# Linear attention followed by an ELU feed-forward layer: batch 0 laid out in slots of two heads by nine tokens, its small matmuls on the array's diagonal quarters, and new orders of work for every batch

## The chip, the cores and the metric

The kernel runs on one core of a Trainium2 chip. The metric is the device time of one launch in microseconds (us). A core has a matrix engine (PE, with its weight loads shown apart as PEld), three engines for elementwise work (DVE, ACT, POOL), a queue engine that issues transfers (SP; ACT and POOL issue some too), and 16 DMA engines that all queues share. Each engine works through its own instructions in program order and waits at a semaphore where an operand is not ready.

## What is computed

The inputs are `q`, `k`, `v` of shape (8 batches, 8 heads, 576 tokens, 64) and two weight matrices of 512x2048 and 2048x512, all float32.

```python
q_s = softmax(q, over the 64 features of a token)
k_s = softmax(k, over the 576 tokens of a head)
kv  = einsum('bhsd,bhse->bhde', k_s, v)          # 64x64 per head
x   = einsum('bhsd,bhde->bhse', q_s, kv)         # put back to (8*576, 512)
h   = x @ w_in
out = where(h > 0, h, exp(min(h, 0)) - 1) @ w_out
```

## The kernel before

**The feed-forward layer** runs in nine rounds of 16 steps. Rounds 0 to 7 take 512 tokens of one batch each; round 8 takes the 64 tokens that each batch has over. A step `(j, s)` issues `hidden` (four matmuls of 128x512 into a bank, L778; exp on ACT, L766; minus one on POOL, L767), `project` of the step three before it (four matmuls, L799) and `elu` (max and min on DVE, L789), in that order. A step with nothing else in it takes 8 matmuls.

**The attention** of batch j+1 is cut into words, and the tables `FIRST` (round 0), `SECOND` (round 1), `LATER` and `CHANGED` put words between the steps: `mid` words behind `hidden`, `end` words behind `project`, `after` words behind `elu`. For q: `qmax` and `qsum` (DVE reductions, L586 and L604, with a reciprocal, L606), `qsub` (subtract, L594), `qexp` (ACT, L600), `qmul` (L618), a transpose (`pturn` on PE, L652, or `turn` by DMA, L634) and `pwide`/`wide` (copy to `QT`, L670, L733). For k: a maximum over tokens, `ksub` (L414, L425), `kexp` (L452). `vconv` casts v (L515). `kv` multiplies (L535, L539), `kfac` divides into `MB` (L552, L566), `att` or `flat` multiplies `MB` with `QT` (L687, L709) and `xc` or `xflat` copies the result to `XT`, which `hidden` of the next round reads. `hold` lets SP wait for the last `hidden` matmul.

**Maxima of k.** From batch 2 on `peak2` (DVE, L367, L374) and `join2` reduce them, and `kout2`/`kin` send them through a scratch tensor in DRAM to all partitions (`NB`). Batch 1 is done otherwise: `kmax2` at the end of `START` (DVE, L299 to L312), then `kturn` (PE, L328), `kacross`, `diag`, `kspread` (PE, L431) and `copy` in round 0. Batch 0, before any feed-forward work can start, goes by the word list `START`: `kraw` copies k into banks by matmuls with the identity (L462, L471), `kmin` adds the negative maxima (L479, L488), `kexp` reads the banks (L502). `warm` issues four matmuls whose result is not used (L924). At its end `h:2:4` and `h:0:2` issue the first two matmuls of the first four steps.

**Layout.** A partition holds four neighbouring tokens of every head, 512 tokens in all (parts A and B, four heads each); the other 64 tokens (part R) lie apart, and are loaded by descriptors of 256 bytes, reduced, transposed and multiplied by words of their own (`qmulr`, `turn:R`, `wide:R`, `rest0`, `rcopy0`). Each `store` of a round sends four tiles of 128 rows; `store_rest` sends round 8.

**Queues.** SP issues the loads in the order of the words; POOL issues `w1` and `w2`, the weight loads. Only `hold` and `await` (L962) keep SP back, else it runs ahead and the transfers queue up.

Of the kernel before, what the change touches and what calls it, by code (L numbers as in the profile page):

```python
# [4 lines left out]
ALU = mybir.AluOpType  # L5
# [12 lines left out]
SR = S - SM  # L18
CUTS = (0, 320, 832, 1344, 1856, 2304)
# [6 lines left out]
EARLY = 4  # L26
OB = (3, 4, 5, 6)
# [19 lines left out]
FIRST = {  # L47
    0: ("", "", ""),
    1: ("", "", ""),
    2: ("qmax:A", "w2:6:8", ""),  # L50
    3: ("qsub:0 w1:12:14", "qsub:1:dve", ""),
    4: ("", "qmax0:R qexp:A w2:8:12", "qsum:A load:Q:1:B qsub0:R"),
    5: ("", "kturn kacross", "qexp0:R qmul:A qsum0:R"),
    6: ("diag", "qmax:C", ""),
    7: ("qsub:D:dve", "kspread qsub:2 w1:14:16", "hold copy load:V:1:RAB"),
    8: ("qexp:C", "qmulr0:gp ksub:1:dve", "ksub:0:dve load:K:2:MR"),
    9: ("pturn:A", "ksub:3 ksub:R", "qsum:C pwide:A:act"),
    10: ("qmul:B:dve pturn0:R kexp:A", "pwide0:R:act", ""),
    11: ("vconv:A:dve", "rest0 w2:12:13 vconv:R", "ksub:2:dve rcopy0:act"),
    12: ("load:Q:2:ABR pturn:B kexp:R vconv:B:gp", "", "load:V:2:MR pwide:B:act"),  # L60
    13: ("kv:A", "kexp:B kfac:A:dve att:0", "xc:0 w2:13:15 w2:15:16 peak2:A"),
    14: ("kv:B kfac:B:dve", "att:1 qmulr:dve peak2:B", "xc:1"),
    15: ("peak2:R join2 att:3 xc:3", "", "turn:R att:2 xc:2 kout2"),
}
SECOND = {
    0: ("qmax:A", "qsub:0:dve qmax:C", "load:Q:2:MR qsub:1"),
    1: ("qexp:A", "qsub:D", ""),
    2: ("qsub:2", "", ""),
    3: ("kin qsum:A", "qmul:0", "qexp:C wide0:R:act"),
    4: ("", "qsum:C", "qmul:1:dve ksub:2:dve"),  # L70
    5: ("", "load:K:2:MR", ""),
    6: ("qmulr:dve ksub:R:dve", "kexp:R qmul:B:dve", "ksub:3:dve"),
    7: ("rest0 turn:A", "rcopy0:dve", "vconv:B"),
    8: ("", "vconv:R ksub:A", "kexp:B peak2:B"),
    9: ("peak2:R kexp:A", "vconv:A:dve", "turn:R peak2:A"),
    10: ("", "", "turn:B join2"),
    11: ("", "kv:AB", "wide:A:gp"),
    12: ("kfac:AB:dve", "wide:R:act", ""),
    13: ("wide:B:gp", "flat:0", "xflat:0:act"),
    14: ("flat:1", "load:V:2:MR xflat:1:dve flat:2", "xflat:2:act"),  # L80
# [36 lines left out]
class Gen:  # L117
# [173 lines left out]
    def kmax(self, b, part, en="dve"):  # L291
# [743 lines left out]
```

## Time and profile before

| what | us |
|---|---|
| median of 3 runs (310.12 to 311.53) | 311.34 |
| the profiled execution | 311.08 |
| its span, first to last instruction | 309.3 |
| first feed-forward matmul (`h:2:4`) | 20.74 |
| first `project` matmul | 26.17 |
| round 0's step 4 begins | 27.20 |
| rounds 1, 2, 3, 4, 5 begin | 55.66, 88.22, 119.95, 151.25, 182.54 |
| last `project` matmul ends | 306.06 |

The profiled execution is 1.8 us longer than its span: what lies around the first and last instruction. A round's beginning is the start of its first L778 matmul on the timeline of PE. In rows of the profile a group has its line, engine, operation, tiles, shapes, count, then busy time and the mean of one, then the idle time of its engine before it and who ended it.

### The profile page before, as it was taken

How to read it: one execution, taken by the hardware profiler on the slowest of the kernel's cores; microseconds unless marked ns; L12 is line 12 of the kernel's file. 1: busy time of each engine (PE TensorE's matmuls, PEld its weight loads, DVE VectorE, ACT ScalarE, POOL GpSimd, SP SyncE). 2: the span in 40 equal slices, each digit the busy share in tenths (PEclk: the TensorE clock that was granted, in tenths of full speed). 3: DMA queues.
4: the chain of work that ended last, by engine and by line, in shares of the span. 5: the costliest groups of instructions: out<-in, count | busy, mean ns of one | idle time of the engine just before them, and what ended most of it. 6: DMA issues, size and time to landing. Idle time of an engine off the chain costs nothing.

```text
span 309.3 us, 4546 instructions
## 1 busy us (share of the span) xinstructions
PE 296.4 (96%) x1601; PEld 237.0 (77%) x1601; DVE 241.8 (78%) x420; ACT 177.3 (57%) x295; POOL 173.6 (56%) x229
## 2 busy tenths in 40 slices
PE   4888998999999999999999999999999999999995
PEld 1456875788878888888888888788888888888884
DVE  6999998999969998999799979997995354335441
ACT  1475785567456755694569547855695543334432
POOL 2988985575546754675467546763676333333440
PEclk9999999999999999999999999999999999999999
DMA  7999999999407986756565666561512030003003
GB/s 238 317 352 328 372 335 306 255 290 236 153 12 228 264 199 159 217 142 179 170 215 145 173 177 200 156 156 44 170 36 42 2 136 0 0 2 137 0 1 136
DMA packets 65607, 51.63 MB, mean 167 GB/s; under 512 B 29360, under 2 KB 58288, under 8 KB 65584
## 3 DMA queue, kind: packets, MB, share of 16 engines
q1 hardware_dynamic: 57984, 41.23, 48.9%
q0 software_dynamic: 6400, 8.39, 10.3%
q10 hardware_dynamic: 1200, 1.72, 1.8%
q8 instruction: 12, 0.20, 0.3%
q14 instruction: 11, 0.09, 0.1%
HBM read 38.27 MB, written 9.45 MB: 154 GB/s over the span
## 4 chain that ended last, share of the span: by engine, by line
PE 86%; DMA 6%; DVE 4%; SPq 1%; ACT 1%; issue 0%; POOL 0%; DVEq 0%
PE bank L778 41%; PE bank L799 40%; DMA KR<-in_k_dram 6%; PE bank L709 2%; PE bank L535 1%; PE bank L687 1%; DVE QZ L604 1%; SPq L276 1%; SPq L284 1%; DVE KA L299 1%; DVE QM L586 0%; DVE KM L367 0%; DVE QS L618 0%; DVE DG L355 0%; DVE MB L566 0%
## 5 line engine op out<-in xcount | busy, mean ns | idle before, releaser
L767 POOL TENSOR_SCALAR ES<-ES 128x512 f32<-128x512 f32 x144 | 95.8, 666 | 118.1 <-ACT ES L766 118.1
L799 PE MATMUL bank<-W2S,GT 128*128 128x512 f32 x576 | 154.7, 392 | 0.9 <-DVE GT L789 0.9
L778 PE MATMUL bank<-XT,W1S 128*128 128x512 f32 x512 | 139.2, 394 | 0.2 <-ACT XT L696 0.2
L789 DVE SCALAR_TENSOR_TENSOR GT<-bank,ES 128x512 fp32r<-128x512 f32 x144 | 96.5, 678 | 50.2 <-PE bank L778 41.5
L766 ACT ACTIVATE ES<-bank 128x512 f32<-128x512 f32 x144 | 85.4, 597 | 86.5 <-PE bank L778 85.8
L799 PEld LDWEIGHTS bank<-W2S,GT 128*128 128x128 f32 x576 | 107.2, 188 | 23.7 <-DVE GT L789 1.4
L778 PEld LDWEIGHTS bank<-XT,W1S 128*128 128x128 f32 x512 | 94.2, 188 | 19.6 <-ACT XT L696 0.9
L594 POOL TENSOR_TENSOR QR<-QR,QM 128x512 f32<-128x512 f32 (+3 forms) x24 | 28.7, 1197 | 5.4 <-DVE QM L586 5.2
L600 ACT ACTIVATE QR<-QR 128x1024 f32<-128x1024 f32 (+3 forms) x18 | 19.0, 1061 | 12.6 <-POOL QR L594 11.3
L586 DVE TENSOR_REDUCE QM<-QR 128x16 f32<-128x1024 f32 (+3 forms) x18 | 21.7, 1207 | 0.6 <-DMA QR<-in_q_dram 0.5
L604 DVE TENSOR_REDUCE QZ<-QR 128x16 f32<-128x1024 f32 (+3 forms) x18 | 21.7, 1204 | 0.0
L731 ACT ACTIVATE XT<-bank 128x512 fp32r<-128x512 f32 (+2 forms) x28 | 15.5, 552 | 10.6 <-PE bank L709 10.6
L414 DVE TENSOR_TENSOR KR<-KR,NB 128x512 f32<-128x512 f32 x25 | 17.7, 739 | 0.2
L778 PE MATMUL bank<-XTR,W1S 128*128 128x512 f32 x64 | 16.6, 389 | 0.0
L367 DVE TRANSPOSE_TENSOR_REDUCE KM<-KR 128x32 f32<-128x1024 f32 x12 | 14.8, 1236 | 1.7 <-DMA KR<-in_k_dram 1.7
L452 ACT ACTIVATE EK<-KR 128x1024 bf16<-128x1024 f32 x14 | 14.7, 1050 | 0.8 <-POOL KR L414 0.8
L618 POOL TENSOR_TENSOR QS<-QR,QI 128x1024 f16<-128x1024 f32 (+1 forms) x9 | 14.5, 1617 | 1.1 <-DVE QI L606 1.1
L778 PEld LDWEIGHTS bank<-XTR,W1S 128*128 128x128 f32 x64 | 12.0, 188 | 2.5
L709 PE MATMUL bank<-QT,MB 128*128 128x320 f32 (+5 forms) x48 | 11.5, 300 | 0.0
L709 PEld LDWEIGHTS bank<-QT,MB 128*128 128x128 f32 x48 | 8.9, 188 | 3.3 <-DVE XT L733 0.5
L809 DVE COPY OSB<-bank 128x512 f32<-128x512 f32 x16 | 10.3, 684 | 0.4 <-PE bank L799 0.4
L618 DVE TENSOR_TENSOR QS<-QR,QI 128x1024 f16<-128x1024 f32 (+1 forms) x9 | 10.4, 1154 | 0.1
(96 smaller groups left out, 205.4 us busy)
## 6 DMA issues: line engine op xcount, KB each, us to landing
out_dram<-OSB SPq DMA_DIRECT2D x35, 256.0 KB, 2.8
KR<-in_k_dram SPq DMA_DIRECT2D x7, 1024.0 KB, 9.4
VR<-in_v_dram SPq DMA_DIRECT2D x6, 1024.0 KB, 7.8
QR<-in_q_dram SPq DMA_DIRECT2D x5, 1024.0 KB, 6.7
W1S<-in_moe_w_in_dram POOLq DMA_DIRECT2D x8, 512.0 KB, 11.4
QR<-in_q_dram SPq DMA_DIRECT2D x6, 512.0 KB, 8.0
VR<-in_v_dram SPq DMA_DIRECT2D x4, 512.0 KB, 8.2
W2S<-in_moe_w_out_dram POOLq DMA_DIRECT2D x3, 512.0 KB, 10.6
```

Source lines behind the costliest of these rows:

```text
L414: self.op(en, lambda: e.tensor_tensor(kv, kv, m, ALU.subtract), keys + ["NB"], keys)
L586: self.op("dve", lambda: v.tensor_reduce(self.QM[:, g], QR[:, g, :], AX.X, ALU.max), self.qkeys(b, part), self.qstat("QM", part))
L594: self.op(en, lambda: e.tensor_tensor(QR[:, g, :], QR[:, g, :], m, ALU.subtract), keys + self.qstat("QM", part), keys)
L600: self.op("act", lambda: a.activation(QR[:, g, :], QR[:, g, :], AF.Exp), keys, keys)
L604: self.op("dve", lambda: v.tensor_reduce(self.QZ[:, g], QR[:, g, :], AX.X, ALU.add), self.qkeys(b, part), self.qstat("QZ", part))
L618: self.op(en, lambda: e.tensor_tensor(out, src, z, ALU.mult), keys + self.qstat("QI", part), [f"QS{x}" for x in cells])
L709: last = pe.matmul(self.bank[bank][:, a - c0:b - c0], self.MB[f][:, :, :].rearrange("p u d -> p (u d)"), self.QT[:, f, a - f * S:b - f * S ...
L766: self.op("act", lambda: a.activation(ES[:, :], ps, AF.Exp), [f"bank{bank}"], [ek])
L767: self.op("gp", lambda: g.tensor_scalar(ES[:, :], ES[:, :], -1.0, 1.0, ALU.add, ALU.mult), [ek], [ek])
L778: return pe.matmul(ps, self.W1S[:, kc, c * 128:(c + 1) * 128], x[:, kc, 0:SM], start=(kc == 0), stop=(kc == 3))
L789: self.op("dve", lambda: v.scalar_tensor_tensor(self.GT[n % NG][:, :], ps, 0.0, ES[:, :], ALU.max, ALU.min), [f"bank{bank}", ek], [f"GT{n ...
L799: return pe.matmul(self.bank[OB[t]][:, :], self.GT[n % NG][:, t * 128:(t + 1) * 128], self.W2S[:, c, :], start=(c == 0), stop=(c == NCH - 1))
```

## The change

- **Layout.** A partition holds nine neighbouring tokens, and 64 partitions a head. For batch 0 a slot holds two neighbouring heads on the two halves of the partitions, one load per slot (descriptors of 2304 bytes) and no part R. For q of later batches a slot holds one head of one pair on each half, loaded by four transfers of 64 partitions. Part R of q is the ninth token; its own words go, except for batch 0's, which still follow in round 0 (`qmax0:R` to `rcopy0`). k and v of later batches keep the old layout.
- **Batch 0.** The maximum of k is one reduction per slot; `kmin` has two matmuls per bank in place of one; `kv` has 72 matmuls of 64x64 in place of 40 of 128x64, each with one half of the partitions in and the same half out; the transposes of q are 64x64 too. `warm` and `await` are no longer in `START`.
- **Batch 1's maxima of k** go by `peak`, `join`, `kout` and `kin` in round 0; `kturn`, `kspread` and `copy` go. Batch 1 uses `flat` and `xflat` at the end of round 0, its rest included, in place of `att` and `xc`, and of `rest0` in round 1.
- **First chunk in halves.** Step 0's exp, minus one and elu work on 256 columns twice, so that `project` of its first two tiles can wait for the first half alone.
- **Stores** of a round send eight transfers of 64 rows. All tables of words are new.

```diff
-START = ("load:K:0:A load:Q:0:A load:K:0:R kmax:A qmax:A load:K:0:B kmax:S kraw:A load:Q:0:B kraw:S "
...
+START = ("load:Q:0:1 qmax:1 load:K:0:1 load:K:0:0 load:K:0:2 qsub:1:gp load:Q:0:0 qexp:1 kmax:1 "
+         "kmax:0 qsum:1 kraw:A load:K:0:3 qmax:0 qsub:0:gp qexp:0 w1:2:4 load:Q:0:2 w1:0:1 kturn:A "
+         "kmax:2 kmax:3 kturn:B load:V:0:2 load:V:0:3 kraw:B qmax:2 qsum:0 load:Q:0:3 kraw:T kraw:S "
+         "load:V:0:1 load:K:1:R kacross:A load:Q:1:0:act diag:act:A load:V:0:0 qsub:2:dve qmax:3 "
+         "vconv:B:act kmin:A kacross:B kmin:S diag:dve:B kmin:T qexp:2 w1:1:2 qsub:3:dve qexp:3 "
+         "qmul:A:dve vconv:A:dve w1:4:6 kexp:A kmin:B kexp:S qsum:2 kexp:B kexp:T kv:A qmul:2:gp "
+         "pturn:A kv:B qsum:3 pwide:1:act kfac:A:act pwide:0:act qmul:3:dve load:K:1:M att:0 xc:0 "
+         "pturn:B kfac:B:act w2:0:3 att:1 load:Q:1:1 w1:6:9 w2:3:5 xc:1 h:2:4 pwide:3:dve att:3 "
+         "pwide:2:act xc:3 w1:9:10 att:2 w2:7:9 h:0:2 w2:5:6 w2:6:7 xc:2 ")
 FIRST = {
...
+    0: ("hold peak:B qmax:A load:Q:1:2", "peak:A peak:R", ""),
     1: ("", "", ""),
...
+    2: ("", "w1:10:13 join load:Q:1:3 qsub:0:dve", ""),
+    3: ("qsub:1", "kout", ""),
+    4: ("qexp:A", "qmax0:R", "qsub0:R qsum:A w2:9:13"),
+    5: ("qmul:A", "", ""),
+    6: ("qexp0:R w1:13:16", "qmax:B qsum0:R kin", ""),
+    7: ("qsub:3", "qmul0:R:dve", "qsub:2:dve pturn:A"),
+    8: ("pwide:A:act ksub:3:dve hold ksub:2:dve", "load:V:1:RAB qexp:B", "ksub:0:dve"),
+    9: ("pturn0:R qsum:B pwide0:R:act", "kexp:B", "ksub:1"),
+    10: ("rest0 rcopy0:act", "load:K:2:MR qmul:B:dve", "ksub:R"),
+    11: ("load:Q:2:0", "vconv:A:dve", "vconv:R vconv:B:dve kexp:A w2:15:16"),
+    12: ("pturn:B pwide:B:act", "", "kexp:R"),
+    13: ("w2:13:15 pturn:R pwide:R:act", "", "kv:AB kfac:AB:dve"),
+    14: ("peak2:A flat:0", "xflat:0:act load:Q:2:1", "load:Q:2:3 flat:1 xflat:1:act peak2:R"),
+    15: ("peak2:B load:Q:2:2 flat:2 load:V:2:MR", "", "xflat:2:act flat:3 xflat:3:act flat:4 xflat:4:act join2 kout2 xrest:gp"),
...
+    def kv_first(self, part, bank):
...
+            for x in range(2 * P, 2 * P + 2):
+                c0 = VW * (x % 2)
+                for r in range(QN):
+                    for a in range(2):
+                        sl = slice(64 * a, 64 * a + 64)
+                        last = pe.matmul(self.bank[bank][sl, c0:c0 + VW], self.EF[sl, r, x, :],
+                                         self.VF[sl, r, x, :], start=(r == 0), stop=(r == QF))
...
+    def kv_fac_first(self, part, bank):
...
+        self.op("dve", lambda: v.reciprocal(z, ps[:, :, 64]), [f"bank{bank}"], [f"KZ{P}"])
+        for a in range(2):
+            sl = slice(64 * a, 64 * a + 64)
+            self.op("dve", lambda: v.scalar_tensor_tensor(
+                self.MBG[sl, 2 * P:2 * P + 2, a, :], ps[sl, :, 0:64], 1.0,
+                z[sl].unsqueeze(2).broadcast_to([64, 2, 64]), ALU.mult, ALU.mult),
...
+    def pieces(self, name, n, count):
+
+        halves = [(slice(256 * i, 256 * i + 256), [f"{name}{n % count}{'LH'[i]}"]) for i in range(2)]
+        return halves if n < FINE else [(slice(0, SM), [k for _, keys in halves for k in keys])]
...
-            self.op("pe", mm, [f"GT{n % NG}", f"W2_{c}"], [f"bank{OB[t]}"])
+            self.op("pe", mm, [f"GT{n % NG}{'LH'[t // 2]}", f"W2_{c}"], [f"bank{OB[t]}"])
```

The new `kfac` words of `START` are always DVE's (`kv_fac_first` has no engine argument): one reciprocal and two multiplications on 64 partitions by 128 columns.

More of the change, by code (lines that the diff above doesn't have):

```diff
@@ L18 @@
 SR = S - SM
+QP = 64
+QN = S // QP
+QF = SM // QP
 CUTS = (0, 320, 832, 1344, 1856, 2304)
@@ L53 @@
[L53 to L60, printed above, removed]
@@ L74 @@
[L74 to L80, printed above, removed]
-    15: ("kout2 flat:3", "xflat:3:dve", "flat:4 xflat:4:act xrest:act qmax2:A"),
+    0: ("qmax:A qsub:1 qmax:B", "", "load:Q:2:2 qsub:0"),
+    1: ("", "qsub:3", "load:K:2:MR"),
@@ L91 @@
[L91 to L99 removed]
+    0: ("", "qsub:0:dve", ""),
```

601 lines of the change are left out of this document (300 added, 301 removed), and 6 rows, old and new, of the table START.

## The prediction

> **What bounds the kernel now.** I read the busy times in stretches cut at the beginnings of the rounds, then PE's and DVE's timelines at the seams.
>
> ```profile
> 16.00:21.00 5.00, 3.73 (x62) 2.55 (x62) 4.89 (x11) 4.10 (x8) 4.97 (x6) 1.00 1.39 359
> 27.20:55.60 28.40, 27.31 (x168) 20.70 (x167) 26.15 (x41) 19.29 (x34) 21.88 (x27) 1.00 1.29 335
> 55.60:88.20 32.60, 32.38 (x181) 25.85 (x181) 30.08 (x57) 18.49 (x31) 19.24 (x23) 1.00 0.83 206
> 151.20:182.50 31.30, 31.30 (x177) 25.74 (x177) 28.36 (x49) 20.50 (x34) 18.84 (x24) 1.00 0.62 177
> ```
>
> Behind the length stand PE, PEld, DVE, ACT, POOL, the clock, the DMA share and GB/s. From round 3 on PE never idles and a round takes 31.3 us: 128 matmuls, started 0.2266 apart (a step of eight is 1.81), are 29.0, attention is 2.3. The change takes no matmul away there. What can move lies before 120 us: the start (first `project` at 26.17), round 0 (28.5 us for its last 12 steps, 21.8 of them feed-forward), round 1 (32.56), round 2 (31.73). In the start DVE is busy 4.9 of 5 us, in round 0 26.15 of 28.4: before 56 us DVE is the queue to follow.
>
> ```profile
> 4.59 3.78 PE L471 MATMUL bank<-KR,ID 128*128 128x512 f32 x4 [4.59 <-DMA KR<-in_k_dram]
> 8.66 2.06 PE L924 MATMUL bank<-GT,ONES 128*128 128x512 f32 x4
> 26.17 1.20 PE L799 MATMUL bank<-W2S,GT 128*128 128x512 f32 x4 [0.94 <-DVE GT L789]
> ...
> 52.74 0.50 PE L687 MATMUL bank<-QT,MB 128*128 128x512 f32 x1 [0.97 <-DVE MB L566]
> ...
> 50.75 1.25 DVE L367 TRANSPOSE_TENSOR_REDUCE KM<-KR 128x32 f32<-128x1024 f32 x1 [1.12 <-DMA KR<-in_k_dram]
> ```
>
> PE waits for the first `elu` (0.94) and in round 0 for `MB` (0.97). The last line is why: DVE stood 1.12 us before batch 2's `peak2`, whose load was late, with `kfac` queued behind.
>
> **The start, by DVE's queue.** The rows I use:
>
> ```profile
> L586 DVE TENSOR_REDUCE QM<-QR 128x8 f32<-128x512 f32 x2 | 1.4, 680 | 0.0
> L604 DVE TENSOR_REDUCE QZ<-QR 128x8 f32<-128x512 f32 x2 | 1.3, 652 | 0.0
> L618 DVE TENSOR_TENSOR QS<-QR,QI 128x1024 f16<-128x1024 f32 x8 | 9.7, 1214 | 0.1
> L515 DVE CAST VB<-VR 128x1024 bf16<-128x1024 f32 x3 | 2.7, 895 | 0.5 <-DMA VR<-in_v_dram 0.5
> L301 DVE TENSOR_TENSOR KT<-KR 128x256 f32<-128x256 f32 x4 | 1.7, 416 | 0.0
> L652 PE MATMUL bank<-ID,QS 128*128 128x128 f16 x32 | 2.5, 221 | 0.8 <-DVE QS L618 0.8
> ```
>
> Landings: before, the first 512 KB are there 3.8 us after issue, at 4.5, and all of k (1.70 MB behind SP) at 8.25, 0.32 MB/us between. After, k is complete with the sixth slot, 1.77 MB: 8.5. `kmax` of a slot reduces 576 elements, 0.75 by the 512-wide row; its strided operand is in no row here, so 0.75 to 1.5. `kmax:3` ends near 9.7. From there DVE has, in order: qmax 0.68, qsum 0.85 (with its reciprocal, 0.20), kacross 0.28, qsub 0.65, qmax 0.68, kacross 0.28, diag 0.42, qsub 0.65, qmul:A 1.21, vconv:A 1.0, two qsum 1.7, kfac:A 0.84 (0.15 and two of 0.345): 9.24, so 18.9; I add 0.5 for the wait for q's last slot (2.95 MB, about 12.5, beside the weights): 19.4, against 19.04 for the first `MB` pair before. Then qmul 0.68, kfac:B 0.84, pwide 0.68: DVE is through at 21.6.
>
> On PE, 20 matmuls of `kv` took 0.5 us before (the two column halves start together); 36 on diagonal quarters are taken at 0.6 to 0.9 by that pitch, bounded by 1.8 if no two overlap. A half's transposes go from 8 at 0.056 to 32: 0.45 (two at once, half the columns) to 1.8. Both lie beside DVE's queue. After `qmul:3` (20.1) follow pturn:B 0.7, att 0.45, xc 0.6, pwide 0.6 and two xc of 0.6 on ACT: the last `XT` at 23.65, against 23.29.
>
> `elu` in halves: before, 2.88 us lay between the last `XT` and `project`; half-size exp (0.38, the 128x256 eviction), minus one (0.37) and elu (0.4) make it about 1.85, so 25.5. But DVE has peak:B 1.24, qmax:A 1.35, peak:A 1.24 and peak:R 0.87 queued ahead of that elu: 21.6 + 4.7 = 26.3, `project` at 26.6. So the first term is **+0.4**, bounds -0.7 (peaks done early) and +3.7 (the weights, below). The removed `warm`, memsets and `await` cost or save nothing on DVE's chain; `warm` is a rival.
>
> **Round 0.** Off PE go batch 1's four k transposes (0.35 between steps) and `kspread` (0.23); the 0.97 wait for `MB` goes, since `kfac:AB` now stands ahead of `peak2`. SP's `hold`, kept at steps 0 and 8, leaves the bytes the same: 16.1 MB to batch 2's k, at 319 GB/s on average about 50 us as before, and `peak2:A` asks for it at step 14, no earlier. What is late next is DVE. From 21.6 to the end of kfac:AB its words are: peaks 3.35, join 1.35, qmax 1.35+0.40+1.35, qsum 1.62+0.59+1.62, qsub 2x0.65, qmul 0.41+1.35, ksub 3x0.69+0.87, vconv 2x0.9, kfac 1.5, 14 elu of 0.68: 30.5; with 0.6 for gaps it ends at 52.7. The same sum for before (from 21.6, kmax2 included) is 29.4, and took 31.1, the 1.12 stall in it; so the sum is good to half a microsecond. `flat:0` can start when the first `MB` is done, 51.7. The five flats share one bank, each behind the copy of the one before: five times 0.45 + 0.6. The fourth input piece of round 1's first matmuls is there near 56.8, against the 56.51 at which PE went on before: **+0.2 for start and round 0 together**. Below it is bounded by PE's own work: 27.6 + 21.8 + 2.9 of attention = 52.3, -3.4. Above: the batch's subtractions on DVE took 1.16 and 1.22 where POOL worked beside them, against 0.68; six more such are +3.
>
> `kin` makes ACT wait for the scratch write; before, that took 5.1 us to land, the read 4.2. `kout` at step 3 and `kin` at step 6 leave some 5.5 us, and `ksub` asks at step 8: no wait to 2 us of DVE, inside the +3.
>
> **Rounds 1 and 2.** Round 1 lies 1.27 above a later round. In it `rest0` goes (0.46, a step of 2.28 against 1.82) and the late `XT` at its start (0.22 plus a restart); the DMA transposes fall from three to two per batch. DVE's sum there is 0.8 larger than before, beside a DVE busy 30.08 of 32.6. **-0.8**, bounds -1.3 and +0.5. Round 2: **-0.2**, bounds -0.4 and +0.5. Rounds 3 to 7 keep 31.3: their words on DVE sum to 28.5 against 30.2, ksub and qmul moving to POOL, busy 18.8 of 31.3. **0**, bounds -0.2 and +1.5. The eight stores (SP, 0.4 each, beside PE) and the end, 3.2 us behind the last matmul, with the same bytes and descriptors: **0**, +-0.2.
>
> Sum: +0.2 - 0.8 - 0.2 = -0.8 on the profiled execution's 311.1, 310.3; that one lay 0.26 below the median, so I say **310.4**.
>
> **Rivals.**
>
> *PE sets round 0 (about 308.1).* If DVE keeps up, because kmax is quick and POOL's share does not slow its subtractions, the two PE waits (0.94, 0.97), the 0.6 of matmuls and round 1's excess all go: -2.0 - 1.0. For it: PE idles 1.1 us in round 0 before. Against it: the sums above.
>
> *PE starts at half speed (about 313.3).* The clock column says 1.00 from the start, but the 512-column matmuls of 4.59 start 0.85 apart and the same ones at 14.03 0.43; `warm` begins 0.42 apart and the next matmul after it runs at full speed, from 10.3, after 5.7 us of unbroken work. After the change `warm` is gone, k comes in four slots, and PE has two pieces of work (about 5.5 to 7.4, 9.7 to 12) with holes, then kmin. If the clock has not risen by 20.8, four att, eight `h` and eight `hidden` matmuls cost 0.2 more each, 4.0, of which some 2.5 are not covered. Against it: the eight kmin:A and kmin:B matmuls now fill 12.4 to 15.8 if slow, which is again an unbroken stretch. The Trainium skill, TensorE: Matmul & The Clock Gate, What's actually happening, says that the array idles at half rate and is released after one busy window of about 3.4 us; by it alone that stretch just suffices, or not, as the window falls. The same page's Part 4 says that transposes do not count as busy, which speaks against the change.
>
> *The second weights come late (about 312.5).* `w2:0:3` is issued behind `qmul:2` on POOL, near 19 (before: `w2:0:2` at 11.2). Weight loads took 6.4 to 14.0 us to land: 25.4 at the least, 29.8 at the median of 10.8, where `project` wants it at 26.6. By bytes (7.7 MB ahead and with it) it is there at 25.1; so a wait only if SP's loads take more than their share. From 26.6 on it delays all behind it.
>
> *The rewritten rounds stall* (an unfit word in rounds 3 to 7, 0.3 us each): +1.5; it is in the bounds.
>
> **Chances.** Forecast 0.47 (own range 309.0 to 311.9), PE sets round 0 0.25, half speed 0.13, late weights 0.15. About 0.5% (1.6 us) is what can be told from no change. Faster: the second and a fifth of the first, less some of the second that stays above 309.8: 0.32. Slower: the third and half of the fourth: 0.21. The rest, 0.47, is the same. The range leaves out the last 0.1 at each end: 307.8 to 313.4.
>
> **What would show it.** DVE ends its start near 21.6; first `project` between 25.5 and 27; PE's 512-column matmuls 0.23 apart at 21 us (else the half-speed rival); no wait of PE for W2S; no idle PE for `MB` over 0.5 us; round 1 begins at 55.3 to 56.5; rounds 1 and 2 near 31.8 and 31.5. A round of 31.6 or more behind 120 us, or a `kmax` of 1.5 us, makes the sum wrong.

## The result, and the profile after

The changed kernel takes **328.9 us** (median of 4 runs, 325.95 to 332.71) against 311.43 for the kernel before, run beside it (4 runs, 310.12 to 312.53). It is slower, and the forecast of 310.4 was wrong. The profiled execution took 332.71, its span is 330.9; it is the longest of the four, 2.1% above the shortest, so the ratio of 1.053 (95% interval 1.044 to 1.063) is that of the other three, 325.95 to 329.98.

In the changed kernel's lines `hidden` is L820, its exp L803, minus one L804, `elu` L831, `project` L840; `qsub` is L620, `qmul` L663, `ksub` L427, the peaks' copies L394 to L405, `MB` L585, `flat` L744, the copies to `QT` and `XT` L767 to L772.

| stage | before | after | longer by |
|---|---|---|---|
| first `hidden` / first `project` | 20.74 / 26.17 | 22.28 / 28.19 | |
| round 0's step 4 begins | 27.20 | 29.19 | 2.0 |
| round 0 from there | 28.46 | 34.02 | 5.6 |
| round 1 | 32.56 | 37.49 | 4.9 |
| round 2 | 31.73 | 33.52 | 1.8 |
| rounds 3, 4, 5, each | 31.30 | 33.28 | 2.0 |
| round 6 | 31.3 | 32.2 | 0.9 |
| round 7 | 29.0 | 29.0 | 0 |

These sum to 21.1, and the last `project` ends 21.1 later; the span is 21.6 longer, since 3.7 us lie behind that matmul in place of 3.2. So there is no one cause: every stage that the new tables order lost something, and only the round with no attention in it did not. The stages are those of the longest execution. In e2, e3, e4 and e6 below, where the words of round 0 are the same, round 0 took 30.9 to 33.9, all at full clock: 2.4 to 5.5 more than before, in place of 5.6. Busy time by stretch, changed kernel (behind the length: PE, PEld, DVE, ACT, POOL, clock, DMA share, GB/s):

```profile
16.00:21.00 5.00, 3.25 (x139) 2.70 (x138) 4.71 (x14) 3.75 (x9) 3.15 (x4) 1.00 1.70 244
29.20:63.20 34.00, 29.75 (x175) 21.29 (x174) 29.29 (x49) 17.29 (x29) 18.22 (x22) 0.95 1.27 298
63.20:100.70 37.50, 34.89 (x178) 27.22 (x177) 28.50 (x53) 19.08 (x30) 19.90 (x23) 0.91 0.62 152
134.22:167.49 33.27, 32.15 (x177) 25.52 (x176) 27.44 (x46) 19.40 (x32) 23.25 (x26) 1.00 0.68 166
234.10:266.20 32.10, 31.61 (x177) 25.52 (x176) 20.96 (x34) 19.42 (x32) 23.20 (x26) 1.00 0.28 60
```

In a later round PE now stands for 1.1 us and its matmuls take 0.85 more (32.15 against 31.30), while POOL's busy time rose from 18.84 to 23.25: work went from DVE (28.36 to 27.44) to POOL at more than it cost. Rounds 0 and 1 show a granted clock below 1. PE's timeline tells where PE waits (start, duration, tiles, and in brackets the wait and who ended it):

```profile
22.28 1.19 PE L820 MATMUL bank<-XT,W1S 128*128 128x512 f32 x4 [1.15 <-ACT QT L767]
28.19 1.17 PE L840 MATMUL bank<-W2S,GT 128*128 128x512 f32 x4 [1.20 <-DMA W2S<-in_moe_w_out_dram]
47.45 1.19 PE L820 MATMUL bank<-XT,W1S 128*128 128x512 f32 x4 [1.95 <-DVE GT L831]
66.93 2.07 PE L840 MATMUL bank<-W2S,GT 128*128 128x512 f32 x4 [2.43 <-DMA W2S<-in_moe_w_out_dram]
157.78 0.41 PE L744 MATMUL bank<-QT,MB 128*128 128x320 f32 x1 [0.47 <-DVE MB L585]
162.62 1.20 PE L820 MATMUL bank<-XT,W1S 128*128 128x512 f32 x4 [0.33 <-DVE GT L831]
```

One line for each stage. At 28.19 `project` waits for the first load of the second weights; at 47.45 the chain of batch 1's maxima (below) has made an `elu` late; at 66.93 it is `w2:13:15`; from 152 on, waits behind POOL. The chain of waits, first from 29 us, then from 150 (start, duration, who):

```profile
28.94 1.81 DVE KC L399
...
31.50 6.12 DMA kmax_scratch<-KU
...
37.64 6.76 DMA NB<-kmax_scratch
...
45.03 1.76 DVE KR L427
46.80 0.61 DVE GT L831
...
55.88 11.01 DMA W2S<-in_moe_w_out_dram
```

```profile
150.34 2.09 POOL QS L663
152.42 0.58 POOL ES L804
153.01 2.09 POOL QS L663
155.09 0.59 POOL ES L804
...
155.78 0.69 DVE GT L831
...
156.86 0.86 DVE MB L585 x3
```

The first: the maxima go 6.12 us to memory and 6.76 back, and DVE's `ksub` is on the chain behind them. The second: two `qmul` of 2.09 on POOL, each ahead of a minus one; `elu`, `kfac` and the first `flat` follow late. `elu` waited 1.44 there. Its row names the `hidden` bank, but the other operand, the minus one, ended at 155.68, just ahead of its start at 155.78.

### The profile page after: what moved, and what is told of

The parts are those of the page before. It is cut to its first block, busy times and chain, and to the rows that moved or that the text cites. A ratio compares the mean times of both kernels' runs of the same rounds, so it can differ in the third digit from the quotient of the medians.

```text
span 330.9 us, 4716 instructions
## 1 busy us (share of the span) xinstructions
PE 303.8 (92%) x1684; PEld 237.5 (72%) x1684; DVE 241.0 (73%) x411; ACT 170.8 (52%) x281; POOL 191.4 (58%) x236
## 4 chain that ended last, share of the span: by engine, by line
PE 48%; POOL 23%; DVE 13%; DMA 10%; ACT 3%; issue 2%; SPq 0%; DVEq 0%
PE bank L820 23%; PE bank L840 22%; POOL ES L804 8%; POOL KR L427 6%; POOL QS L663 5%; POOL QR L620 4%; DMA W2S<-in_moe_w_out_dram 3%; DVE GT L831 3%; DMA NB<-kmax_scratch 2%; DVE QM L611 2%; PE bank L744 2%; DMA kmax_scratch<-KU 2%; DMA QW<-QS 2%; ACT ES L803 1%; DMA KR<-in_k_dram 1%
## 5 line engine op out<-in xcount | busy, mean ns | idle before, releaser
L840 PE MATMUL bank<-W2S,GT 128*128 128x512 f32 x576 | 157.4, 397 | 4.3 <-DMA W2S<-in_moe_w_out_dram 3.6
L804 POOL TENSOR_SCALAR ES<-ES 128x512 f32<-128x512 f32 (+1 forms) x145 | 94.5, 656 | 114.5 <-ACT ES L803 114.2
L820 PE MATMUL bank<-XT,W1S 128*128 128x512 f32 x512 | 141.8, 399 | 4.2 <-DVE GT L831 3.1
L831 DVE SCALAR_TENSOR_TENSOR GT<-bank,ES 128x512 fp32r<-128x512 f32 (+1 forms) x145 | 97.1, 676 | 66.4 <-PE bank L820 45.2
L803 ACT ACTIVATE ES<-bank 128x512 f32<-128x512 f32 (+1 forms) x145 | 84.8, 591 | 99.5 <-PE bank L820 86.5
L840 PEld LDWEIGHTS bank<-W2S,GT 128*128 128x128 f32 x576 | 108.1, 190 | 27.5 <-DMA W2S<-in_moe_w_out_dram 2.7
L820 PEld LDWEIGHTS bank<-XT,W1S 128*128 128x128 f32 x512 | 95.0, 190 | 27.8 <-DVE GT L831 6.6
L620 POOL TENSOR_TENSOR QR<-QR,QM 128x576 f32<-128x576 f32 (+2 forms) x24 | 26.7, 1123 | 6.0 <-DVE QM L611 6.0
L663 POOL TENSOR_TENSOR QS<-QR,QI 128x1152 f16<-128x1152 f32 (+1 forms) x13 | 26.5, 2039 | 4.7 <-DVE QI L650 4.6
L643 ACT ACTIVATE QR<-QR 128x1152 f32<-128x1152 f32 (+2 forms) x19 | 19.2, 1010 | 13.6 <-POOL QR L620 12.7
L427 POOL TENSOR_TENSOR KR<-KR,NB 128x512 f32<-128x512 f32 (+1 forms) x17 | 25.8, 1518 | 0.2 <-DMA NB<-kmax_scratch 0.2
L611 DVE TENSOR_REDUCE QM<-QR 128x18 f32<-128x1152 f32 (+2 forms) x19 | 21.6, 1140 | 0.4 <-DMA QR<-in_q_dram 0.3
L648 DVE TENSOR_REDUCE QZ<-QR 128x18 f32<-128x1152 f32 (+2 forms) x19 | 21.8, 1150 | 0.0
L767 ACT ACTIVATE XT<-bank 128x512 fp32r<-128x512 f32 (+2 forms) x28 | 15.2, 544 | 11.4 <-PE bank L744 11.3
L744 PE MATMUL bank<-QT,MB 128*128 128x320 f32 (+5 forms) x56 | 14.5, 320 | 5.4 <-DVE MB L585 2.3
L744 PEld LDWEIGHTS bank<-QT,MB 128*128 128x128 f32 x56 | 10.0, 187 | 12.8 <-DVE MB L585 6.5
L820 PE MATMUL bank<-XTR,W1S 128*128 128x512 f32 x64 | 16.6, 389 | 0.0
L820 PEld LDWEIGHTS bank<-XTR,W1S 128*128 128x128 f32 x64 | 12.0, 188 | 2.5
L462 PE MATMUL bank<-KR,ID 128*128 128x512 f32 (+1 forms) x12 | 6.1, 655 | 6.5 <-DMA KR<-in_k_dram 6.5
## 6 DMA issues: line engine op xcount, KB each, us to landing
VR<-in_v_dram SPq DMA_DIRECT2D x6, 1024.0 KB, 11.1
```

The source lines that it names most:

```text
L427: self.op(en, lambda: e.tensor_tensor(kv, kv, m, ALU.subtract), keys + ["NB"], keys)
L611: self.op("dve", lambda: v.tensor_reduce(self.qview(self.QM[:, :], b, part), QR, AX.X, ALU.max, negate=self.negated(b, part)), self.qkeys( ...
L620: self.op(en, lambda: e.tensor_tensor(QR, QR, m, how), keys + self.qkeys("QM", b, part), keys)
L643: self.op("act", lambda: a.activation(QR, QR, AF.Exp), keys, keys)
L648: self.op("dve", lambda: v.tensor_reduce(z, QR, AX.X, ALU.add), self.qkeys(f"QR{b % 2}", b, part), self.qkeys("QZ", b, part))
L663: self.op(en, lambda: e.tensor_tensor(out, QR, z, ALU.mult), reads, keys)
```

## The experiments

The edits are given in words of the tables (- taken out, + put in), all against the changed kernel. Each time is that of a single execution unless an interval is given; the changed kernel's own runs lie up to 6.8 us apart, so I compare stages, and totals only where an interval stands beside them.

**The weights.** Theory: two words stand too late on POOL's queue.

```diff
 e1_w2_early, FIRST:   9 mid  + w2:13:15        13 mid  - w2:13:15
 e2_first_w2, START:   "w1:1:2" + "w2:0:3" behind it;  "kfac:B:act" - "w2:0:3" behind it
```

> The changed kernel with one word moved: the load of the second weights' chunks 13 and 14 (w2:13:15) goes from the middle of step 13 of round 0 to the middle of step 9. In the changed kernel it was issued at 55.88 us and landed at 66.89; the project of chunk 13 waited for it, and TensorE ran at half speed from 65.77 to 72.60. Theory (the late load is the cause, the half speed follows from TensorE's idle time): issued about 42, landed by 55, no wait of project for W2S at chunk 13, no half-speed stretch at 66 to 72, and round 1 takes about 32.5 in place of 37.5 us; the whole run about 5 us less. Rival (the half speed comes by itself, whatever TensorE waited for): only the wait of 2.4 us goes, round 1 takes about 35. Round 0 stays near 34.0 from its step 4, rounds 2 to 5 near 33.3.

> The changed kernel with the first load of the second weights (w2:0:3) issued ahead of the first weights' chunks 4 and 5 and ahead of GpSimd's qmul:2, at about 12.5 us in place of 18.84; chunks 4 and 5 of the first weights then at about 13.3. Theory (the first project at 28.19 waited for this load, landed 28.05): the load lands by 25 to 26, the first project begins at 27.1, when the first half of its elu is done, and round 0 begins about 1 us earlier. Rival (the project is held by the elu or by the sequence of TensorE): the first project stays at 28.0 to 28.3. The first hidden matmul stays at 22.3, since it waits for the first weights' chunk 2, issued at 10.06 as before. Rounds 2 to 5 unchanged at 33.3.

e1 took 325.3, span 323.5. `w2:13:15` was issued at 45.14, landed at 53.27, and round 1 shrank from 37.5 to 32.2:

```profile
61.01:93.20 32.19, 32.19 (x177) 25.22 (x176) 27.91 (x52) 19.35 (x30) 19.17 (x23) 1.00 0.75 188
```

PE is busy for all of it at full clock. The other runs with the word left in its place have 34.8 to 37.5 there, those with the edit 32.2 (33.5 in x7, below; why is open). So round 1's whole loss is that one transfer, and without it the round is 0.4 shorter than before. e2 took 331.0, span 329.2: `project` came at 27.25 in place of 28.19, without the wait (`[...]` is gone), right behind the first half of its `elu`:

```profile
27.25 1.20 PE L840 MATMUL bank<-W2S,GT 128*128 128x512 f32 x4
```

But round 1 began only 1.0 earlier, at 62.2, which is no more than the runs differ by. The theory held for the cause of the wait.

**The later rounds.** Theory: POOL's queue; rival: ScalarE's `kout2`, or the order of the flats.

```diff
 e3_kout_late, LATER:    12 after - kout2               14 after + kout2
 e4_qmul_behind, LATER:  8 mid - qmul:B   9 end - turn:B   10 mid + qmul:B turn:B
 e6_rebalanced, LATER:   1 after qsub:1 -> DVE   5 after ksub:2 -> DVE   6 mid ksub:3 -> DVE
                         3 mid - vconv:A (DVE)  7 mid + vconv:A (ACT)   11 mid - qmax2:A  13 after + qmax2:A
```

> The changed kernel with ScalarE's issue of the peaks' way out (kout2) moved in rounds 2 to 5 from behind step 12 to behind step 14; the peaks themselves stay where they are. Rival theory of the loss (ScalarE, which stood from 160.87 to 163.85 us in round 3 until the join was done, brings the exp of step 13 late): rounds 2 to 5 lose about 1.1 us less each, 32.2 in place of 33.3. Main theory (VectorE's queue sets the time: two qmax, a peak and the join stand ahead of the elu of steps 11 and 12 there, and the chain begins late because GpSimd's two qmul hold up the minus-one): rounds 2 to 5 stay at 33.1 to 33.3.

> The changed kernel with GpSimd's second qmul (qmul:B, 2.13 us) moved in rounds 2 to 7 from the middle of step 8 to the middle of step 10, behind the minus-one of steps 9 and 10, and the transpose of its result (turn:B) with it. Main theory (the two qmul in GpSimd's queue bring the minus-one of step 9 to 155.05 us in round 3, hence the elu of step 9 to 155.78, the factors and the first flat matmul to 157.78): that elu begins 1.2 to 1.4 us earlier in its round, the idle of 0.47 us ahead of the first flat matmul goes, VectorE's queue behind it moves up, and rounds 2 to 5 take 31.4 to 32.0 in place of 33.3, round 6 31.4 in place of 32.2. Rival (it is VectorE's own load there, or ScalarE's wait for the peaks, that sets the time): at most 0.9 us goes, rounds 2 to 5 stay at 32.4 or above. The whole run 5 to 9 us less by the main theory, 2 to 4 by the rival.

> The changed kernel with work of rounds 2 to 7 given back by GpSimd: qsub:1 (where VectorE idles early in the round), ksub:2 and ksub:3 go to VectorE, VectorE's conversion of V (vconv:A) goes to ScalarE ahead of its exp of the keys' half B, and the reduction qmax:A moves from step 11 to step 13. GpSimd's busy time in a round falls from 23.3 to about 19.5 us, VectorE's rises from 27.4 to about 28.5. Theory (GpSimd is saturated from 138 to 155.7 us of round 3, its minus-one of step 9 is late, and the chain elu, factors, first flat matmul and VectorE's queue behind them with it): the minus-one of step 9 ends about 0.9 us earlier in the round, no idle of TensorE ahead of the first flat matmul, no wait of hidden 14 for the elu, rounds 2 to 5 take 31.4 to 32.1 in place of 33.3, round 6 31.4 to 31.8 in place of 32.2. Rival (the way through the transposing DMA into the wide copy sets the first flat matmul, or VectorE's load does): rounds 2 to 5 stay at 32.5 or above.

e3 took 330.65 and left rounds 2 to 5 at 33.3 to 33.6: ACT's wait for the maxima fell as a cause. e4 took 325.68, rounds 2 to 5 32.3 to 33.2: the first `flat` no longer waits, but another does, since the transposing DMA behind the later `qmul` lands late:

```profile
151.96 0.30 PE L744 MATMUL bank<-QT,MB 128*128 128x320 f32 x1
157.28 0.48 PE L744 MATMUL bank<-QT,MB 128*128 128x320 f32 x2 [1.14 <-POOL QT L769]
```

That is 0.0 to 1.0 less per round, half of what the theory asked at best, and but for round 5 (32.34) in the rival's band. e6 took 323.59: rounds 3 to 6 are 31.83, round 2 32.4.

```profile
130.36:162.19 31.83, 31.83 (x177) 25.48 (x176) 28.27 (x49) 20.52 (x33) 19.92 (x23) 1.00 0.71 174
```

POOL is back at 19.92, PE is never idle. So 1.5 of the later rounds' 2.0 goes with these five words. Three of them leave POOL; the other two move `vconv:A` from DVE to ACT and put one of DVE's reductions two steps later. That POOL's queue is the cause fits e4 and the chain above, but how much of the 1.5 is POOL's alone was not separated. The 0.5 left (31.83 against 31.30) is matmuls that start further apart.

**Round 0.** Theory: the maxima's way through memory, and POOL holding DVE up; rivals: DVE's own peaks, or too many words on DVE and POOL.

```diff
 e5_krow:     3 end  kout -> krow (NB read from batch 1's first row of keys)   6 end - kin
 x1_qsub_dve: 3 mid  qsub:1 -> qsub:1:dve
 x6_no_peaks: e5, and - peak:A peak:B peak:R join
```

e5 and x6 shift batch 1's keys by its first row in place of its maxima (x6 leaves the maxima out).

> The changed kernel, in which batch 1's shift (the row that is taken off its keys before the exponential) is read in step 3 of round 0 from the first row of its keys in memory, and not from the peaks: batch 1's way out and back through memory (kout at 31.50 to 37.62, kin at 37.64 to 44.40 us in the changed kernel) is left out. VectorE's peaks and join of batch 1 stay as work, their result is not used; batches 2 to 8 are as before. Theory (this way is what costs round 0: ScalarE stands 4.0 us until the join is done, and VectorE 2.6 us for NB with the elu of step 8 behind it): NB lands before 40 us, ScalarE's stand at 28 to 31.5 goes, the step from hidden 5 to 6 falls from 2.8 to about 2.1 us and that from 10 to 11 from 3.4 to 4.8 to about 2.3, and round 0 takes 29.5 to 30.8 in place of 31.5 to 34.0. Rival (VectorE's and GpSimd's words of round 0 are too many, whatever NB does): step 10 to 11 falls by at most 0.5 us and round 0 stays at 31.3 or above. Rounds 2 to 5 unchanged at 33.3.

> The changed kernel with one word of round 0 moved from GpSimd to VectorE: qsub:1 of step 3 (128x576, 1.16 us on GpSimd). In the changed kernel one of the join's copies of 32x16 elements, 0.16 us as a rule, took 1.81 us and ended 0.04 us after GpSimd's qsub:1 did. Theory (VectorE's small copy does not get on while GpSimd's tensor operation runs, so that the two hold each other up): the three copies take 0.15 to 0.35 us each, the join ends at about 30, kout is issued 1.5 us earlier, ScalarE's stand of 4.0 us falls to about 2.5, and hidden 6 begins at 32.0 to 32.8 in place of 33.81 (counted for a start of round 0 at 29.19). Rival (the copy waits for something else, its input or its turn): the copy stays at 1.5 us or more, and hidden 6 at 33.4 or later, since VectorE has 0.70 us more to do. Rounds 1 to 8 as in the changed kernel.

> The run with batch 1's shift read from the first row of its keys, in which batch 1's peaks and their join (some 5 us of VectorE's work in steps 0 to 2 of round 0) are now left out as well, since nothing uses them. Theory (VectorE's work and the way through memory together are what batch 1's shift costs round 0): the step from hidden 5 to 6 falls to 2.2 or less, round 1 begins at 57.5 to 58.8 us in place of 59.66 in that run and 60.6 to 63.2 in the runs with the way through memory. Rival (the order of batch 1's other words, above all the exponential of half B ahead of the rest's copy and the turns that wait for qmul, holds the end of round 0): round 1 begins at 59.2 or later.

e5 took 326.92: round 0 30.6, in the theory's band, with round 1 from 59.7. But with the same words of round 0 and the way through memory left in, e2, e3, e4 and e6 took 30.9 to 33.9 and began round 1 at 60.6 to 62.6, so the length alone decides nothing; only the start of round 1, 0.9 ahead of the earliest, speaks for the theory. Step 10 to 11 kept its 3.4 us, the rival's point. PE's and ACT's timelines:

```profile
44.34 0.63 PE L781 MATMUL bank<-QT,MB 128*128 128x64 f32 x4 [0.87 <-ACT QT L772]
```

```profile
42.36 1.17 ACT L648 ACTIVATE QR<-QR 128x1152 f32<-128x1152 f32 x1 [1.52 <-DVE QR L625]
43.91 0.38 ACT L772 ACTIVATE QT<-bank 128x256 fp32r<-128x256 f16 x1
```

PE waits for a small copy to `QT`, which stands in ACT's queue behind `qexp:B`, which waited 1.52 for a subtraction of DVE's. x1 shows the other half. The changed kernel, then x1, DVE's three copies of 32x16:

```profile
28.60 2.34 DVE L399 COPY KC<-KC 32x16 f32<-32x16 f32 x3
```

```profile
29.05 1.03 DVE L399 COPY KC<-KC 32x16 f32<-32x16 f32 x3
```

With `qsub:1` off POOL, the copy of 1.81 takes 0.16; it had stood beside POOL's subtract of 128x576. (The copy behind it now takes 0.50, beside POOL's minus one.) Step 5 to 6 fell to 1.81, as the theory asked. But step 7 to 8 rose to 3.37 (`pturn:A` now waits for `qmul:A`), and x1 took 329.35: what was won at one wait was lost at the next. x6 (329.33) freed DVE, busy 23.93 of 30.02:

```profile
29.71:59.73 30.02, 27.39 (x176) 20.67 (x175) 23.93 (x40) 16.94 (x29) 17.83 (x22) 1.00 1.24 302
```

Round 1 began at 59.7 again, as in e5. That is the rival's band (59.2 or later). In x6 `kfac:AB` ended at 54.52, in e5 at 54.45, although e5 has some 5 us more of DVE's words ahead of it. The peaks' cost on DVE is not what is left, and my suspicion of DVE as the queue of round 0 fell with it.

**The start.** Theory: q's early transfers slow the weights.

```diff
 e7_weights_first: e2, and load:Q:1:0 load:Q:1:1 held until batch 0's last qmul (await)
```

> The changed kernel with the first load of the second weights ahead of the first weights' chunks 4 and 5 (as in the run with that edit alone) and, besides, the two loads of batch 1's Q (Q:1:0 from ScalarE at 10.16 us, Q:1:1 from SyncE at 9.33) held on SyncE's queue until the first qmul is done, at about 16 us. Theory (these two megabyte-halves went ahead of the weights and took some 3 us of the transfers): the first weights' chunk 2, landed 22.23, lands at 19 to 20; the first hidden matmul begins at 20.7 to 21.0, when the first XT is ready, the last XT is at 23.5 to 24.0 in place of 24.82, the first project begins at 25.7 to 26.3, round 0 begins 1.9 to 2.4 us earlier than at 29.19. Rival (TensorE and VectorE set the last XT, not the weights): the first hidden matmul is earlier but the first project stays at 27.0 or above.

The weights did land early (19.23), but `project` came at 30.74: above 27.0, as the rival says, but for a reason that it does not name. The expectation calls the two held loads halves of a megabyte; they are 288 KB each. DVE's timeline:

```profile
26.93 1.35 DVE L611 TENSOR_REDUCE QM<-QR 128x18 f32<-128x1152 f32 x1 [3.05 <-DMA QR<-in_q_dram]
30.26 1.35 DVE L831 SCALAR_TENSOR_TENSOR GT<-bank,ES 128x256 fp32r<-128x256 f32 x3
```

`qmax:A` of batch 1 stands ahead of the first `elu` and waited 3.05 for its late load. e8, the same with the first chunk whole, was idle at the same place and tells nothing (329.29). What e7 does tell: its step 4 began 2.6 later than the changed kernel's, and its round 1 still at 61.5, 1.7 earlier and inside the 60.6 to 62.6 of the runs above. The start does not set the end of round 0.

**Together.** c11 is e1, e2 and e6 without `qsub:1` on DVE in `LATER`; x3 is e1, e2 and e6 with `qsub:1` on DVE in `FIRST` too, and `ksub:3/2/0` behind the `elu` of step 8, `rest0` at step 11. c9 is c11 with e7's hold and most of batch 1's words in round 0 about one step later (with `qmax:A` at step 1, so that no `elu` waits behind it); c10 is c9 with the first chunk whole.

```diff
 x3_waits_out, FIRST:  3 mid qsub:1:dve   8 mid - ksub:3 ksub:2   8 after + ksub:3:dve ksub:2:dve ksub:0:dve
                       10 mid - rest0 rcopy0    11 mid + rest0 rcopy0
 c9_combined, FIRST:   4 mid kout  7 mid kin  9 mid qexp:B  9 after ksub:3 ksub:2  11 mid qmul:B
 x4_round0:     x3, later ksubs, qexp:B at 8 mid, qmul:B on POOL, batch 1's vconv on ACT, qsub:3 earlier, pturn:A later
 x5_turn_later: x3, pturn:A and pwide:A one step later, ksubs after step 9, qmul0:R on POOL
 x7_no_peaks_waits_out: x3 with x6's edit
```

> The changed kernel with three of the edits tried alone, together: the load of the second weights' chunks 13 and 14 at step 9 of round 0, the first load of the second weights ahead of the first weights' chunks 4 and 5, and GpSimd's ksub:2 and ksub:3 on VectorE, vconv:A on ScalarE, qmax:A at step 13 in rounds 2 to 7 (qsub:1 stays on GpSimd). Theory (the losses are of separate places and add): round 0 begins at 28.3, takes 31.5 to 32.5, round 1 32.2, round 2 32.2, rounds 3 to 5 31.5 to 31.7, round 6 31.5 to 31.7; the span is 315 to 317 in place of 330.9. Rival (they share a cause, so that one gives back what the other takes): the span stays above 318.

> The changed kernel with all edits that took a loss away alone, and none of those of the combined run that brought a wait back: the load of the second weights' chunks 13 and 14 at step 9 and their first load ahead of the first weights' chunks 4 and 5; rounds 2 to 7 as in the rebalanced run; in round 0 qsub:1 on VectorE, the three subtractions that need NB behind the elu of step 8, and the small rest product from step 10 to step 11. Theory: round 0 begins at 28 (27.5 to 28.5), takes 29.5 to 31.0, round 1 32.2, round 2 32.3, rounds 3 to 6 31.8, so that the span is 313 to 316 in place of 330.9, and what is left against the kernel before (309.3) is round 0 with 1 to 2.5 us, the start with 0.5 to 1 and rounds 2 to 6 with 0.5 each. Rival (round 0's work is too much for VectorE and GpSimd in any order): round 0 stays at 32 or above, the span at 317 or above.

> The run with three edits together with these besides: batch 1's first two Q loads held until the first qmul is done, the reduction qmax:A of batch 1 moved from step 0 to step 1 of round 0, behind the first elu (where it stood in the way of the run with the weights first); kout from step 3 to step 4 behind qexp:A, kin from step 6 to 7; qexp:B behind the copy of the transposed rest, the subtractions that need NB from step 8 behind the elu of step 9, the small rest product from step 10 to 11. Theory (what round 0 still loses beyond the weights are three waits of the in-order queues: ScalarE's for the join, VectorE's for NB, TensorE's for the rest's copy behind qexp:B): the first project begins at 26.3 to 27.2, no wait of ScalarE over 2 us at 28 to 32, the step from hidden 10 to 11 at 2.4 or less, round 0 takes 28.8 to 30.2. Rival (round 0 is bound by the sum of its work on VectorE and GpSimd, and a wait that is removed comes back at the next word): round 0 stays at 31.0 or above. The span by the theory 311 to 313.5.

> The run with the waits taken out, with round 0 eased for VectorE, which was busy 30.9 of the 32.3 us there (26.2 of 28.5 in the kernel before): qmul:B of round 0 goes from VectorE (1.85 us there) to GpSimd, the conversions of V (0.70 and 0.69 us) to ScalarE, GpSimd's qsub:3 from step 7 to step 6, so that VectorE's small qmul0:R does not lie beside it (2.2 us in place of 0.4), the turn of half A from behind step 7 to step 8, and the words behind it by half a step. Theory (round 0 is bound by VectorE's work and the standing still of its instructions beside GpSimd's): VectorE's busy time in round 0 falls below 28.5 us, TensorE's wait of 1.1 us at the turn of half A goes, and round 0 takes 29.5 to 31.0 in place of 32.3. Rival (the chain of batch 1's qsub, qexp, qsum, qmul and turn, or the waits for memory, set it): round 0 stays at 31.8 or above although VectorE is less busy. Start and rounds 1 to 8 as in the run with the waits taken out.

> The run with the waits taken out, with four words of round 0 changed: batch 0's small qmul0:R from VectorE to GpSimd (on VectorE it took 2.2 us beside GpSimd's qsub:3 instead of 0.4), the turn of half A from behind step 7 to step 8 behind the project (TensorE waited 1.1 us for GpSimd's qmul:A there), the three subtractions that need NB from step 8 to behind step 9, and the turn and copy of the rest from step 9 to 9 and 10. ScalarE's qexp:B stays behind step 8, unlike in the run with VectorE eased, where it stood 4.2 us in ScalarE's queue. Theory (round 0's loss is of words that stand a step too early for their inputs in in-order queues, and of VectorE standing still beside GpSimd): the step from hidden 7 to 8 falls from 3.5 to 1.8 to 2.4, the step from 10 to 11 stays at or below 2.4, and round 0 takes 29.8 to 31.3 in place of 32.3; the span is 314.5 to 316.5. Rival (whatever wait is removed there, the chain of batch 1 gives it back at its next word): round 0 stays at 31.8 or above, the span at 317 or above.

> The run with the waits taken out, with batch 1's shift read from the first row of its keys and batch 1's peaks and join left out: the start, round 0 and rounds 2 to 7 all without what was found. Theory (the way through memory and VectorE's work are the rest of round 0's loss): round 0 takes 29.0 to 30.3 in place of 32.3, round 1 begins at 57 to 58.3 (55.66 in the kernel before), the span is 314 to 315.5. Rival (the words' order): round 0 stays at 31 or above.

| | step 4 | round 1 begins | round 0 | round 1 | rounds 3 to 5 | span |
|---|---|---|---|---|---|---|
| c11 | 27.71 | 61.40 | 33.7 | 32.2 | 32.0 | 318.1 |
| x3 | 28.02 | 60.28 | 32.3 | 32.2 | 31.8 to 32.7 | 317.2 |
| c9 | 28.35 | 64.28 | 35.9 | 32.2 | 32.0 | 321.0 |
| c10 | 27.95 | 63.28 | 35.3 | 32.2 | 32.0 | 320.0 |
| x4 | 28.42 | 64.64 | 36.2 | 32.2 | 31.8 | 320.6 |
| x5 | 28.91 | 63.84 | 34.9 | 32.2 | 31.8 to 32.7 | 320.9 |
| x7 | 28.11 | 60.60 | 32.5 | 33.5 | 31.8 to 32.2 | 318.3 |

Behind round 0 the parts add: c11 (319.98, span 318.1) has e1's round 1 (32.2), and its rounds 3 to 6 lie some 0.2 above e6's. Its span is above the 315 to 317 expected and just in the rival's band (above 318), since round 0 took 33.7 and so gave the start's gain back. x3 is the best version, 320.77 (median of 6 runs, 318.93 to 321.42; before 311.04, ratio 1.0316, interval 1.0293 to 1.0340). Of the 21.6 us of span between the profiled executions 13.7 are regained, of the 17.5 between the medians about 8. Its round 0 (32.3) and span (317.2) lie in the rival's bands all the same. It still loses to the kernel before; no version here beats it. x5 is 321.12 (4 runs, ratio 1.0305, interval 1.0271 to 1.0338), the same within the intervals.

Round 0 stayed at 32 or more in every combined run, which is what the rivals of c9, x4, x5 and x7 said, and each shift moved the wait. In c9, c10, x4 and x5 part of it (3.4 to 6.8 us) ran at half clock. x4's DVE was busy for 28.8 of 36.2 us, so it was not short of time. PE in c9, x4 and x5:

```profile
51.72 0.62 PE L694 MATMUL bank<-ID,QS 128*128 128x128 f16 x8 [3.02 <-DVE QS L663]
```

```profile
45.02 0.31 PE L691 MATMUL bank<-ID,QSR 64*64 64x64 f16 x8 [3.39 <-ACT QT L767]
```

```profile
44.55 0.42 PE L691 MATMUL bank<-ID,QSR 64*64 64x64 f16 x8 [2.95 <-ACT QT L767]
```

In c9 the transposes wait for a late `qmul:B` on DVE; in x4 and x5 for a copy to `QT` in ACT's queue. In x5 it stood behind `kin`, where ACT waited 3.6 us until `kout` had landed, and behind `qexp:B`, which waited 1.99 more; in x4 behind `qexp:B` too, which waited 4.21 for a subtraction on DVE:

```profile
42.31 1.16 ACT L643 ACTIVATE QR<-QR 128x1152 f32<-128x1152 f32 x1 [4.21 <-DVE QR L620]
...
43.86 1.01 ACT L767 ACTIVATE QT<-bank 128x1024 fp32r<-128x1024 f16 x1
```

x7 took 320.12 and kept a round 0 of 32.5 though it has no way through memory and no peaks; there DVE waits 1.5 us for V of batch 1. From c10 against c9 the halves can be priced: from the last `XT` to the first `project` 2.30 us with them, 2.98 whole. But c10's first `project` came 0.4 earlier than c9's (26.91 against 27.31), not 0.5 to 0.9 later as expected, because its first `hidden` came 1.1 earlier: a gain at the start of round 0 is not shown.

## Why the prediction was wrong, point by point

- **The start, "+0.4": it was +2.0.** The rival of the late second weights happened: `w2:0:3` issued at 18.84, landed at 28.05, and PE idled 1.20 for it; e2 removes that. `kv` (0.76) and the transposes (0.70) were right; `kmax` took 1.13, inside 0.75 to 1.5. The end of DVE's queue (21.52 against 21.6) was right by luck: `kmax:3` ended at 11.1 in place of 9.7, and the words behind it took 10.4 us in place of 11.9. `w1:2:4` landed at 22.23 (before 18.42), which together with a copy to `QT` made the first `hidden` 1.5 late. The half-speed rival did not occur: PE is at full clock from 11.2, and its `hidden` matmuls from 25.2 to 26.6 start 0.23 apart.
- **"+0.2 for start and round 0 together": it was +7.6, outside the bound of +3** (+4.9 to +7.0 in e2, e3, e4 and e6). The step that failed is that DVE's words alone give the end of `kfac:AB` (52.7) and this the end of the round. It ended at 57.98, and 54.45 to 54.52 in e5 and x6, whether or not DVE had 5 us of peaks ahead of it; batch 1's words stand in ACT's and POOL's queues as much. Two terms in it were too small. One is "no wait to 2 us of DVE" for `kin`: I gave `kout` at step 3 and `kin` at step 6 some 5.5 us and took the landing times of a quieter stretch (5.1 and 4.2). Here they were 6.12 and 6.76, begun late by the 1.81 copy, and DVE waited 2.56, with an `elu` queued behind its `ksub`. The other is the five flats: `flat:0` began behind the last `MB` (58.03 behind 57.98) and not behind the first, and they came some 1.2 apart, not 1.05; so 5.2 us lie between the end of `kfac:AB` and round 1, where the forecast has 3.2 (52.7 to 55.9). Of the 5.6 in round 0 about 1.7 is the half clock at 48.7 (PE busy 29.75 against 27.8 to 28.3 in the runs with full clock), which came 1.3 us behind the wait at 47.45 and in none of e1 to e6.
- **"Round 1 -0.8": it was +4.9.** Without the late `w2:13:15` it is -0.4 (e1), inside my bounds. The failed step is what I did not write: I priced late weights for the first load only, and never walked POOL's queue for the others. `w2:13:15` is issued behind the minus one of step 13, at 55.88, and took 11.0. The wait itself was 2.43 in the longest place; with the clock at half from 65.8 to 72.6 the round lost 5.3. In e7 the same wait left the clock at full, and the round took 34.8: 2.6 more than e1's.
- **"Rounds 3 to 7: 0", round 2 -0.2: it was +6.9 and +1.8.** "their words on DVE sum to 28.5 against 30.2, ksub and qmul moving to POOL, busy 18.8 of 31.3" summed one engine's words only. POOL's price for a moved word is higher (`qmul` 2.09 against 1.35 on DVE, `ksub` 1.29 to 1.73 against 0.68 to 1.10), it rose to 23.25, and an average share of 0.7 says nothing where a word stands ahead of a minus one that the next `project` needs. "The rewritten rounds stall" was put at 0.3 each; it was 2.0.
- **Right:** round 7 and the layout's small matmuls. **Right in part:** the end came out 0.5 longer (3.7 in place of 3.2 behind the last matmul), outside +-0.2; e6 and x3 have 3.2. The `elu` in halves is worth 0.68 of the 1.0 it was given; its first half was done at 27.07, forecast 26.3.
- **A slip of the sum:** 310.3 and 0.26 make 310.5, not 310.4; nothing hangs on it.
- The sign said it itself: "A round of 31.6 or more behind 120 us" was to make the sum wrong, and rounds 3 to 5 took 33.3.

**Open:** about 4 us of the start and round 0 (59.7 without the way through memory against 55.66). For that way, 0.9 to 3.5 us is an estimate (59.7 against 60.6 to 63.2 in the runs with round 0's order kept, whatever their start), of one execution each. Of the 4 us, 2.2 lie behind `kfac:AB`: from its end to round 1 it is 5.2 us in every run with the new tables (57.98 to 63.21, in e5 54.45 to 59.66), 3.0 before (52.69 to 55.66). In e5 the first and the last of the flats wait like this:

```profile
54.51 0.41 PE L749 MATMUL bank<-QT,MB 128*128 128x320 f32 x1 [0.44 <-DVE MB L590]
...
59.35 0.47 PE L749 MATMUL bank<-QT,MB 128*128 128x448 f32 x1 [0.69 <-ACT XT L772]
```

No run changed these flats, which hold the rest's share too, so that their price was not tested. Which of batch 1's words or loads sets the other 1.8, that is the end of `kfac:AB`, was not settled: every order tried put the wait elsewhere.

## What to carry to other kernels

Sum the words of every engine that gains work, at that engine's own price, and walk its queue step by step for what stands behind each new word; an average share of 0.7 hid a loss of 2 us per round here. Walk each DMA-issuing queue too: the load that was late here took 11.0 us and was issued 8.6 us before PE stood still for it, and it cost more than its wait, since the clock fell after it. When taking a wait out gains nothing at the end of the stage, look for the next wait before blaming the first.

## What the runs showed of the hardware

- **DVE and POOL hold each other up.** A DVE copy of 32x16 took 1.81 in place of 0.16 and ended with POOL's 128x576 subtract; in x3 a DVE multiplication took 2.20 (0.41 in the changed kernel) beside another, and POOL's minus one 1.27 in place of 0.62 beside a DVE subtract. x1 took the first away by moving POOL's word. The Trainium skill, SBUF — State Buffer, Who interferes with whom, says that DVE instructions with two operands in that memory, and copies in their two-port mode, contend with POOL for a shared port pair, and that for the two-port mode whoever issues first holds it and the other blocks. The traces agree that the two hold each other up, with these numbers. They do not bear out the order: by the profile the copy began 0.02 us and the multiplication 0.16 us ahead of POOL's minus one, and both stood until POOL's subtract behind it was done. In which mode the copy ran no trace shows.

```profile
38.44 2.20 DVE L663 TENSOR_TENSOR QSR<-QR,QI 128x256 f16<-128x256 f32 x1
```

- **The clock falls after shorter holes than I had thought.** The changed kernel, stretches around the two falls:

```profile
45.40:48.70 3.30, 1.35 (x6) 1.05 (x6) 3.30 (x4) 1.86 (x4) 1.09 (x2) 1.00 1.11 335
48.70:52.10 3.40, 3.40 (x9) 1.88 (x8) 3.37 (x6) 2.35 (x4) 1.53 (x3) 0.50 1.14 315
62.40:65.80 3.40, 1.60 (x5) 0.86 (x5) 3.23 (x9) 1.59 (x3) 1.00 (x3) 1.00 1.17 260
65.80:69.20 3.40, 2.27 (x5) 1.82 (x6) 1.21 (x2) 0.00 (x0) 2.26 (x3) 0.50 1.10 247
```

Each fall to 0.50 follows a stretch of 3.3 to 3.4 us in which PE was busy for 1.35 and 1.60, with no single idle time over 1.95 and 2.43; in e5 it fell at 61.99 with none over 1.46. The Trainium skill, TensorE: Matmul & The Clock Gate, HAM oscillation — how this bites in real kernels, asks for no idle gap over some 3.4 us. Here less than that sufficed, and the measurement decides. Nor does the length of the hole decide alone: in e7 PE was busy for 0.17 of the 3.41 us up to 30.74, and the clock stayed at 1.00.

- **Transfers under load.** The 2 KB of the maxima took 6.1 us to land and the 256 KB read 6.8, in a round that moved 298 GB/s. From 16 to 21 us the DMA engines moved 244 GB/s in the changed kernel and 236 to 279 in the other runs that issue batch 1's first two loads of q near 10 us; they moved 340 in e7, e8 and c9, where these two are issued near 17. Why was not tested. e7:

```profile
16.00:21.00 5.00, 4.30 (x117) 3.51 (x116) 4.77 (x12) 3.91 (x9) 2.62 (x4) 1.00 1.85 340
```
